# When weights are converted and gated-unit blocks are issued, in a fused attention, gated unit and soft mixture kernel

## The chip, the cores and the metric

The kernel runs on one core of a Trainium2 chip. The metric is the device time of one execution in microseconds, lower is better. Before the change the median of three runs is 917.54 us (913.38 to 921.64).

## The reference, cut to what matters

Four batches of eight heads: queries are averaged in pairs along the sequence, then ordinary attention follows. Its output is the input of a gated unit, and that feeds a soft mixture of eight small networks.

```python
q_pool = q.reshape(B, H, S // 2, 2, D).mean(axis=3)        # 4, 8, 576, 64
scores = scale * q_pool @ k.T                              # 576 x 1152 for each head
attn = softmax(scores); x = attn @ v                       # 2304 tokens x 512
g = x @ w_gate; h = g * sigmoid(g) * (x @ w_val)           # 512 -> 1536
y = h @ w_out                                              # 1536 -> 512
logits = y @ phi                                           # 2304 x 32 slots
# softmax over tokens gives slot inputs, over slots gives the combination
slot_out = relu(slot_input @ w1[e]) @ w2[e]                # 8 networks, 512 -> 1024 -> 512
out = softmax(logits, axis=1) @ slot_out
```

The weights of the gated unit arrive as 64-bit floats; the kernel turns them into 32-bit and then into a pair of 16-bit numbers (a high and a low part).

## The kernel before, in words

**Attention.** The heads are worked in 16 pairs, counted here from 0 to 15 as in the code (`steps`; four pairs make a batch). For each pair the keys, queries and values are loaded (`load_pair`, line 168), split into 16-bit high and low parts and put in place by transfers of SP's queue (`split_pair`, line 210: QD, KK, QQ, KL, QH). The row maxima of a pair's scores are found during the pair before it: PE computes scores once (line 323), DVE reduces them (lines 329, 338, 341), and one transfer of ACT's queue brings them into QH (line 347). Then each of 21 units computes scores in PE (lines 413, 414), ACT takes the exponential (line 419), POOL or DVE subtracts the high half to get the low half PL (line 426), and PE multiplies with the values (lines 457 to 459). Which PL goes to DVE, and which unit stays in 32 bits, is given for each pair by `DVE_PART` (line 33, six entries) and `F32_PART` (line 51, five entries). At the end of each head `finish` normalises (line 487), and `turn` sends the pair's result through a transposing transfer (line 528) into the operand xT of the gated unit. The buffer `xhl` between the two is single. xT of block j lies in place j mod 4 (`xt_tile`, line 466), so that block 5 takes over the place of block 1.

**The gated unit** works in nine blocks of 256 tokens (`moe_stream`, line 924), each in six slices of 256 columns of the weights (`block_slice`, line 671): 48 matmuls on PE, 16 each on lines 685, 689 and 690, then ACT and DVE for the activation, and small matmuls for the logits. A block can start when its tokens are ready (two blocks after each batch of four pairs), a slice when its weights are converted (`moe["w"]`).

**The conversion** has 36 portions (`prep`): 12 of w_out (`prep_wo`, line 613) and 24 of the other two weights (`prep_w`, line 647). Each loads its part by SP's queue, ACT does two steps (lines 600, 601), and DVE assembles the bits (line 603). A portion of w_out is also stored, transposed in PE and multiplied with phi; a portion of the other two is cast in ACT (line 653) and its low half subtracted in POOL, for the first three in DVE (line 655). A set of six portions makes one slice of weights ready. When the last is issued, three loads of 1024 KB follow (line 902).

**What sets the order.** The program is written out in full by Python loops; the main loop goes through the steps of a pair (42 of them) and after each one issues what is due: maxima, then slices of the gated unit up to a pace, then portions of the conversion up to a pace. A scheduler then orders the instructions of each engine by these priorities; within an engine and within SP's queue they run in that order. The paces are the subject of the change. A block counts 31 parts (`QPB`). If the weights or tokens for the next part are not there, the loop goes on, and the parts are made up for as soon as they are. Six blocks are issued beside attention and three after it; then come the slot networks and the output.

Of the kernel before, what the change touches and what calls it, by code (L numbers as in the profile page):

```python
# [45 lines left out]
MOE_LEAD = 6  # L46
PB, LAG = 6, 3
MOE_START = 4
N_MOE = 6.1
PREP_BEG, PREP_END = 1, 7  # L50
F32_PART = [0.17, 0.0, 0.17, 0.25, 0.33]
VRB = 2
HNB = 1
# [11 lines left out]
def tile_pool_attention_glu_softmoe(  # L65
# [35 lines left out]
    def ps(tag, shape, dtype=F32, bufs=1, name=None):  # L101
        return psum.tile(shape, dtype, tag=tag, bufs=bufs, name=name or tag)
# [50 lines left out]
    steps = [(b, p) for b in range(B) for p in range(NP)]  # L153
# [14 lines left out]
    def load_pair(b, p):  # L168

        r = slice(D if (b, p) == steps[0] else 0, P)  # L170
        kr = at.tile([P, S], F32, tag="kraw", bufs=1, name=f"kr{b}_{p}")
        nc.sync.dma_start(out=kr[r], in_=kT[b, p, r])
        qr = at.tile([P, 2, SQ], F32, tag="qraw", bufs=1, name=f"qr{b}_{p}")
        nc.sync.dma_start(out=qr[r], in_=qT[b, p, r])
        vr = at.tile([P, 2, NCH, D + 1], F32, tag="vraw", bufs=VRB, name=f"vr{b}_{p}")
        nc.sync.dma_start(out=vr, in_=vP[b, p])
        raw[b, p] = (kr, qr, vr)
# [179 lines left out]
    def later(n, fn):  # L357

        due.append((now[0] + n, fn))

    def tick(n=1):
        now[0] += n
        while True:
            run = [d for d in due if d[0] <= now[0]]
            if not run:
                return
            due.remove(run[0])
            run[0][1]()
# [18 lines left out]
    def maxima(n):  # L387
        while n_rm[0] < min(n, MX0 + MXP * (len(steps) - 1)):
            next(maxs)
            n_rm[0] += 1  # L390
# [488 lines left out]
    def load(n, mark=None):  # L879
        key = order[n]  # L880
        ts = place(n, "_".join(map(str, key)))
        m = NQ // len(ts)

        piece[key] = [ts[e // m][:, e % m] for e in range(NQ)]
        for i, t in enumerate(ts):
            if key[0] == "w2":
                _, z, g, c = key
                k = HALF // ZW[z]
                t = t.rearrange("p e (c d) -> p e c d", c=k)
                for e in range(m):  # L890
                    src = w2[NQ * g + i * m + e, c * P:(c + k) * P, Z0[z]:Z0[z] + ZW[z]]
                    dma = nc.sync.dma_start(out=t[:, e], in_=src.rearrange("(c p) d -> p c d", p=P))
                    if mark and e >= Y5E:
                        after(dma, mark)
                continue
            if key[0] == "wo":
                src = wo_d[key[1] * NQ * P:(key[1] + 1) * NQ * P, :].rearrange("(c p) d -> p c d", p=P)
            else:
                e = slice(NQ * key[1] + i * m, NQ * key[1] + (i + 1) * m)
                src = w1[e, key[3] * P:(key[3] + 1) * P, key[2] * HALF:(key[2] + 1) * HALF]  # L900
                src = src.rearrange("e p f -> p e f")
            dma = nc.sync.dma_start(out=t, in_=src)
            if mark:
                after(dma, mark)
# [51 lines left out]
    moe_work = moe_stream()  # L956
    UNITS = 2 * (2 * NCH + 3)
    QPB = 5 * (NF // 2) + 1
    n_moe = QPB * N_MOE / (len(steps) - MOE_START)
    n_done = 0  # L960
    for i, (b, p) in enumerate(steps):
        for u, _ in enumerate(attn(b, p)):
            tick()
            f = (u + 1) / UNITS
            if u == (SPLIT0 if i == 0 else 0):
                if i + 1 < len(steps):
                    split_pair(*steps[i + 1])
                if i + 2 < len(steps):
                    later(0 if i == 0 else LOAD_LAG, lambda k=i + 2: load_pair(*steps[k]))

            if i:
                maxima(MX0 + MXP * i + int(MXP * min(1.0, max(0.0, f - MX_BEG) / (MX_END - MX_BEG))))
            else:
                maxima(9 + int((MX0 - 9) * min(1.0, f / MX0_END)) + int(MXP * min(1.0, max(0.0, f - MX1_BEG) / (MX1_END - MX1_BEG))))
            while i >= MOE_START and n_done < (i + f - MOE_START) * n_moe:
                if not next(moe_work, False):
                    break
                n_done += 1
            while prep and n_prep - len(prep) < (i + f - PREP_BEG) * n_prep / (PREP_END - PREP_BEG):
                prep.pop(0)()  # L980
                if not prep:
                    for n in range(NEE):
                        load(n)
# [25 lines left out]
    t = ps("st", [P, NF // 2, 2, NS], bufs=STB, name="gt")  # L1009
# [7 lines left out]
    t = ps("mm", [P, DM], bufs=MMB, name="si4p")  # L1017
# [11 lines left out]
    t = ps("tr", [P, ND, NS], bufs=TRB, name="siTp")  # L1029
# [44 lines left out]
    for g in range(E // NQ):  # L1074
        for h in range(2):
            t = ps("st", [P, HALF], bufs=STB, name=f"hp{g}_{h}")
# [9 lines left out]
            t = ps("mm", [P, NQ, P], bufs=MMB, name=f"hTp{g}_{h}")  # L1086
# [119 lines left out]
```

## Time and profile before

| | |
|---|---|
| median of three runs | 917.54 us |
| profiled execution | 913.91 us, span 912.1 us |
| granted TensorE clock, mean | 0.964 |
| busy: PE, DVE, POOL, ACT | 823.9, 579.6, 444.5, 357.5 us |
| bytes moved | 134.69 MB, 148 GB/s |

Busy time is the time in which an engine had an instruction in work; matmuls overlap each other, so a busy PE is not a PE at its peak. The granted clock is a share of 2.4 GHz; a mean below 1 means that for part of the stretch the engine ran at 1.2 GHz. A stretch of a pair is counted here from the start of the last normalisation of the pair before it (line 487) to that of its own; the last one, of pair 15, starts at 722.3 us.

### The profile page before, as it was taken

The numbers are of one execution on the slowest core, as the hardware profiler recorded it, in microseconds if no ns is written. First come the engines' busy times: TensorE is split into PE (matmuls) and PEld (weight loads), VectorE is DVE, ScalarE is ACT, GpSimd is POOL, SyncE is SP. The second block draws the span as 40 slices with busy tenths as digits, with TensorE's granted clock in tenths as the row PEclk, the third lists the DMA queues.
The fourth block names the chain that finished last, engine by engine and source line by source line (L and its number), as shares of the span: only waits on it lengthen the run. The fifth ranks groups of instructions, "written<-read, shape, count | busy, mean of one in ns | idle before, by whom it ended". The sixth has DMA issues, their size and how long they took to land.

```text
span 912.1 us, 23728 instructions
## 1 busy us (share of the span) xinstructions
PE 823.9 (90%) x9954; PEld 582.6 (64%) x9954; DVE 579.6 (64%) x1083; ACT 357.5 (39%) x682; POOL 444.5 (49%) x384
## 2 busy tenths in 40 slices
PE   3869789899887899999999998989999999998897
PEld 1445466577655577676767675767677787676445
DVE  6878677764987356677867775786672454444313
ACT  2437576664756233332433334224333322112112
POOL 8646685736689422835765677257556400000100
PEclk9989799799999899999999999999999999999999
DMA  6558858665878612615262625142411199248999
GB/s 174 157 137 232 180 161 246 156 200 131 258 185 249 177 52 25 167 25 143 56 156 42 168 45 136 36 108 38 83 25 37 37 292 333 56 140 204 280 291 290
DMA packets 154267, 134.69 MB, mean 148 GB/s; under 512 B 83632, under 2 KB 123120, under 8 KB 154160
## 3 DMA queue, kind: packets, MB, share of 16 engines
q1 hardware_dynamic: 152000, 133.13, 55.5%
q8 instruction: 78, 1.28, 0.6%
q10 hardware_dynamic: 2160, 0.04, 0.1%
q14 instruction: 29, 0.24, 0.1%
HBM read 84.10 MB, written 7.86 MB: 101 GB/s over the span
## 4 chain that ended last, share of the span: by engine, by line
PE 68%; DVE 16%; DMA 10%; issue 2%; ACT 2%; SPq 1%; POOL 0%; DVEq 0%; ACTq 0%; POOLq 0%
PE st L414 6%; PE st L413 6%; PE mx L323 5%; PE g L685 5%; PE v L685 5%; PE g L689 5%; PE g L690 4%; PE v L690 4%; PE v L689 4%; DMA QH<-mt 4%; DVE mp L329 3%; PE pv L457 3%; PE pv L458 3%; PE pv L459 3%; PE hp L1079 2%
## 5 line engine op out<-in xcount | busy, mean ns | idle before, releaser
L426 POOL TENSOR_TENSOR PL<-P 128x512 f16<-128x512 f32 (+1 forms) x295 | 323.1, 1108 | 234.6 <-ACT P L419 231.3
L419 ACT ACTIVATE P<-st 128x512 f32<-128x512 f32 (+1 forms) x336 | 189.8, 581 | 237.2 <-PE st L414 179.0
L329 DVE TENSOR_REDUCE mp<-mx 128x1 f32<-128x512 f32 x270 | 179.2, 683 | 58.3 <-PE mx L323 57.1
L414 PE MATMUL st<-QH,KL 65*128 65x512 f16 (+1 forms) x576 | 148.3, 296 | 9.8 <-DMA QH<-mt 9.4
L413 PE MATMUL st<-QQ,KK 128*128 128x512 f16 (+1 forms) x576 | 147.7, 293 | 6.8 <-ACT P L419 6.6
L457 PE MATMUL pv<-VV,P 128*128 128x65 f16 x1088 | 141.5, 194 | 1.1 <-DVE x L489 1.0
L458 PE MATMUL pv<-VV,P 128*128 128x64 f16 x1088 | 140.8, 196 | 0.0
L459 PE MATMUL pv<-VV,PL 128*128 128x65 f16 x1088 | 138.1, 193 | 3.0 <-DVE PL L426 2.7
L685 PE MATMUL g<-xT,wgv 128*128 128x256 f16 x432 | 120.1, 278 | 9.0 <-DVE hs L697 7.5
L323 PE MATMUL mx<-kh,QD 128*128 128x512 f16 x270 | 106.5, 414 | 22.0 <-DVE mp L329 12.7
L457 PEld LDWEIGHTS <-P 128*128 128x128 bf16 x1088 | 105.0, 99 | 24.5 <-issue 4.3
L689 PE MATMUL g<-xT,wgv 128*128 128x256 f16 x432 | 120.1, 278 | 0.0
L690 PE MATMUL g<-xT,wgv 128*128 128x256 f16 x432 | 120.0, 278 | 0.0
L685 PE MATMUL v<-xT,wgv 128*128 128x256 f16 x432 | 118.8, 275 | 0.2 <-DVE hs L697 0.2
L689 PE MATMUL v<-xT,wgv 128*128 128x256 f16 x432 | 118.5, 274 | 0.0
L690 PE MATMUL v<-xT,wgv 128*128 128x256 f16 x432 | 118.5, 274 | 0.0
L459 PEld LDWEIGHTS <-PL 128*128 128x128 f16 x1088 | 104.6, 100 | 19.1 <-DVE PL L426 3.5
L458 PEld LDWEIGHTS <-P 128*128 128x128 bf16 x1088 | 104.1, 99 | 12.0 <-issue 1.0
L685 PEld LDWEIGHTS <-wgv 128*128 128x128 f16 x864 | 86.0, 100 | 29.5 <-issue 6.9
L689 PEld LDWEIGHTS <-wgv 128*128 128x128 f16 x864 | 85.4, 99 | 21.6 <-issue 7.1
L690 PEld LDWEIGHTS <-wgv 128*128 128x128 f16 x864 | 85.5, 99 | 18.0 <-issue 0.8
L414 PEld LDWEIGHTS <-KL 65*128 65x128 f16 x576 | 52.8, 99 | 37.5 <-issue 23.2
(177 smaller groups left out, 1224.6 us busy)
## 6 DMA issues: line engine op xcount, KB each, us to landing
w<-in_w SPq DMA_DIRECT2D x16, 1024.0 KB, 7.6
w<-in_w SPq DMA_DIRECT2D x64, 256.0 KB, 5.4
vr<-in_vP SPq DMA_DIRECT2D x16, 585.0 KB, 6.2
KK<-kh SPq DMA_DIRECT2D x62, 144.0 KB, 3.3
qr<-in_qT SPq DMA_DIRECT2D x15, 576.0 KB, 5.8
kr<-in_kT SPq DMA_DIRECT2D x15, 576.0 KB, 4.7
r<-in_w_out SPq DMA_DIRECT2D x12, 512.0 KB, 4.1
r<-in_w_gate SPq DMA_DIRECT2D x24, 256.0 KB, 4.9
```

What stands on the lines that cost most here:

```text
L323: nc.tensor.matmul(t, q, kh[:, k0:k0 + kw], start=True, stop=True)
L329: nc.vector.reduce_max(out=mp[:, g, c:c + 1], in_=t, axis=AX.X)
L413: nc.tensor.matmul(t[:, o:o + w], KK[:, k], QQ[:, q0:q0 + w], start=True, stop=False)
L414: nc.tensor.matmul(t[:, o:o + w], KL[:, k], QH[:, q0:q0 + w], start=False, stop=True)
L419: marks.append(nc.scalar.activation(P32[:, :o], t[:, :o], AF.Exp, scale=1.0 / 16.0).ins.name)
L426: eng.tensor_tensor(out=PL[:, :o], in0=P32[:, :o], in1=PH[:, :o], op=ALU.subtract)
L457: nc.tensor.matmul(dst[:, :D + 1], PH[:, q], VV[:, c, 0, :], start=first, stop=False, skip_group_check=True)
L458: nc.tensor.matmul(dst[:, :D], PH[:, q], VV[:, c, 1, :D], start=False, stop=False, skip_group_check=True)
L459: nc.tensor.matmul(dst[:, :D + 1], PL[:, q], VV[:, c, 0, :], start=False, stop=(c == NCH - 1), skip_group_check=True)
L685: mm = nc.tensor.matmul(o, w[:, 0, d, f], xh, start=(d == 0), stop=False)
L689: nc.tensor.matmul(o, w[:, 0, d, f], xl, start=False, stop=False)
L690: nc.tensor.matmul(o, w[:, 1, d, f], xh, start=False, stop=(d == ND - 1))
```

## The change: two paces

The conversion's pace starts at pair 2 and ends with pair 7, where it started at pair 1 and ended with pair 6. It stays at six portions per pair. The gated unit's pace was 6.1 blocks in equal shares over pairs 4 to 15 (0.51 per pair); now one block is due over pairs 4 to 7 (0.25 per pair) and 5.1 over pairs 8 to 15 (0.64 per pair). What is computed, and the order within the gated unit and within the conversion, stay the same.

```diff
 MOE_START = 4
-N_MOE = 6.1
-PREP_BEG, PREP_END = 1, 7
+
+MOE_PACE = [(4, 0.0), (8, 1.0), (16, 6.1)]
+PREP_BEG, PREP_END = 2, 8
...
     QPB = 5 * (NF // 2) + 1
-    n_moe = QPB * N_MOE / (len(steps) - MOE_START)
+
+    def moe_due(t):
+        for (t0, m0), (t1, m1) in zip(MOE_PACE, MOE_PACE[1:]):
+            if t < t1:
+                return QPB * (m0 + (m1 - m0) * (t - t0) / (t1 - t0))
+        return QPB * MOE_PACE[-1][1]
+
...
-            while i >= MOE_START and n_done < (i + f - MOE_START) * n_moe:
+            while i >= MOE_START and n_done < moe_due(i + f):
```

## Rows read from the trace of the kernel before

**Rows 1.** The page's totals: engine, busy us, share of the span, instructions.
```profile
PE 823.9 (90%) x9954; PEld 582.6 (64%) x9954; DVE 579.6 (64%) x1083; ACT 357.5 (39%) x682; POOL 444.5 (49%) x384
```

**Rows 2.** Busy time by stretch: pairs 1 to 7, pair 11, 8 to 15, after.
```profile
core 0: us, PE busy (x) PEld busy (x) DVE busy (x) ACT busy (x) POOL busy (x), PEclk, DMA share, GB/s
...
57.40:98.80 41.40, 29.99 (x409) 18.73 (x408) 34.42 (x61) 26.68 (x50) 22.71 (x18) 0.87 0.64 175
98.80:141.60 42.80, 37.75 (x411) 23.91 (x411) 27.70 (x53) 26.89 (x53) 32.57 (x26) 0.80 0.71 177
141.60:175.00 33.40, 29.01 (x369) 19.34 (x362) 27.17 (x46) 22.76 (x45) 22.10 (x16) 0.88 0.84 230
175.00:226.20 51.20, 49.90 (x562) 38.68 (x562) 30.19 (x53) 30.14 (x57) 27.66 (x22) 0.98 0.64 171
226.20:261.60 35.40, 32.23 (x461) 22.96 (x460) 31.13 (x55) 23.04 (x46) 23.80 (x19) 1.00 0.67 204
261.60:311.10 49.50, 38.38 (x472) 25.51 (x472) 33.08 (x51) 27.29 (x53) 40.23 (x33) 0.92 0.87 241
311.10:369.50 58.40, 58.40 (x717) 44.47 (x716) 35.00 (x72) 17.23 (x35) 18.98 (x17) 0.98 0.24 48
510.80:550.40 39.60, 38.08 (x501) 27.42 (x499) 31.73 (x52) 15.47 (x29) 29.93 (x25) 1.00 0.46 109
369.50:722.30 352.80, 339.73 (x4401) 246.97 (x4400) 239.78 (x435) 126.67 (x241) 215.27 (x182) 0.99 0.35 82
722.30:845.00 122.70, 113.95 (x1051) 89.01 (x1051) 57.52 (x130) 24.43 (x48) 0.00 (x0) 0.99 0.72 198
```

**Rows 3.** Line 685 by stretch: pairs 4 to 7, pair 11, pairs 8 to 15.
```profile
175.00:226.20 51.20, 16.53 (x61) 6.11 (x61) 0.98 0.64 171
226.20:261.60 35.40, 5.24 (x20) 1.87 (x19) 1.00 0.67 204
261.60:311.10 49.50, 5.62 (x19) 2.09 (x20) 0.92 0.87 241
311.10:369.50 58.40, 26.66 (x96) 9.61 (x96) 0.98 0.24 48
510.80:550.40 39.60, 10.09 (x37) 3.51 (x36) 1.00 0.46 109
369.50:722.30 352.80, 107.82 (x391) 38.73 (x391) 0.99 0.35 82
```

**Rows 4.** The chain of waits within pair 1 (57.4 to 98.8 us), shares by line.
```profile
by line: DVE mp L329 18.7%; DVE r L603 11.9%; DMA QH<-mt 8.7%; PE st L414 7.1%; DVE PL L426 6.2%; DVE mp L338 5.7%; DMA QH<-qh 5.6%; PE mx L323 4.8%; PE st L413 4.7%; DVE wgv L655 4.6%; issue 3.7%; DVE kh L184 3.2%; DVE xhl L499 2.9%; PE wo
```

**Rows 5.** POOL's groups over the span: count, busy us, mean ns, idle before.
```profile
L426 POOL TENSOR_TENSOR PL<-P 128x512 f16<-128x512 f32 (+1 forms) x295 | 323.1, 1108 | 234.6 <-ACT P L419 231.3 <-PE pv L458 1.6 <-POOL PL L426 0.3
...
L236 POOL TENSOR_TENSOR kl<-kr,kh 128x1152 f16<-128x1152 f32 (+1 forms) x16 | 40.4, 2526 | 17.3 <-DVE kh L184 11.0 <-DMA QH<-qh 3.6 <-DVE rs L487 1.5
...
L655 POOL TENSOR_TENSOR wgv<-r,wgv 128x512 f16<-128x512 f32 x21 | 27.7, 1320 | 10.2 <-ACT wgv L653 10.2
```

**Rows 6.** Line 603 on DVE in pairs 2 and 6: busy us and count.
```profile
98.80:141.60 42.80, 4.68 (x6) 0.80 0.71 177
...
261.60:311.10 49.50, 6.83 (x5) 0.92 0.87 241
```

**Rows 7.** DVE's longest waits in pair 6 (261.6 to 311.1 us).
```profile
DVE qh L184 <- DMA QH<-qh: 6.9, 1, 6.9
DVE qr L227 <- DMA qr<-in_qT: 6.7, 1, 6.7
```

**Rows 8.** PE in the second block (start, us), and the logits' groups over the span.
```profile
341.79 0.27 PE L690 MATMUL v<-xT,wgv 128*128 128x256 f16 x1
...
343.10 0.27 PE L690 MATMUL v<-xT,wgv 128*128 128x256 f16 x1
...
L729 PE MATMUL lp<-hs,W2S 128*64 128x256 bf16 x108 | 18.0, 297 | 1.9 <-ACT hs L717 1.6 <-DVE xT L184 0.3
...
L734 PE MATMUL lp<-hs,W2S 128*32 128x256 f16 x108 | 16.8, 283 | 0.4 <-DVE hs L719 0.4
```

## The prediction

> **What bounds the kernel now.** I read the engines' totals first [rows 1]: PE is busy for 90% of the span and no other engine for more than 64%. That share is an average over stages with different limits, so I then cut the span into one stretch per pair of heads (0 to 15), from the start of one pair's last normalisation on line 487 to the next one's [rows 2]. The reader is to see three regimes there. In pairs 1 to 3 PE is idle for 11.4, 5.1 and 4.4 us and its granted clock is 0.87, 0.80 and 0.88: part of the time it ran at 1.2 instead of 2.4 GHz. These pairs hold attention and conversion and no matmul of the gated unit. In pairs 4 to 6 the conversion goes on beside some slices of the gated unit. From pair 7 on the conversion is over and PE is the bound: in pair 7 it is busy for all 58.4 us, in pairs 8 to 15 for 339.7 of 352.8.
>
> How much of the gated unit lies in each stretch is read from the matmuls of line 685, of which a slice (a sixth of a block) has 16 [rows 3]: 61, 20, 19 and 96 in pairs 4 to 7, that is 3.8, 1.25, 1.2 and 6.0 slices. The first block is held up by its weights, which come one slice per pair; the second then runs in one go in pair 7. Pairs 8 to 15 have 391/16 = 24.4 slices, and what is left of nine blocks of six, 17.4, comes after the last pair.
>
> In pair 1 the path that set the end runs through DVE, not PE [rows 4]: the bit assembly of the conversion (line 603) is 11.9% of the chain and its subtraction (line 655) 4.6%.
>
> **The change part by part.** The conversion keeps its 36 portions but starts and ends a pair later; the gated unit keeps its order and its total, and 6 of 12 slices of pairs 4 to 7 go to pairs 8 to 15. I sum against the profiled execution: span 912.1 us, its own time 913.9, which is 3.6 below the median 917.54.
>
> *Pair 1 loses the conversion.* With it go a sixth of everything: 12 transfers on SP's queue (two loads and two stores of w_out, eight loads of the other weights), ACT's two steps and its cast per portion, DVE's line 603, three subtractions and PE's transposes of w_out. The chain's 16.5% of 41.4 us is 6.8 us; with the ACT steps and transposes that stand in the same chain I take 8.0, which brings the pair to the 33.4 that pair 3 takes. Bounds: 0, if attention's own waits take its place, and 11.4, all of PE's idle time. Late next is attention's own DVE work, the maxima of line 329, already 18.7% of the chain.
>
> *Pairs 2 and 3* convert before and after. Pair 2 takes over the three subtractions that go to DVE, 4.6% of pair 1's chain or 1.9 us: between 0 and 1.9, taken as 1.
>
> *Pairs 4 to 7* took 51.2 + 35.4 + 49.5 + 58.4 = 194.5 us. Now each has a sixth of the conversion and 1.5 slices. A slice beside attention is priced by pair 7 against pair 11 [rows 2, 3], both without conversion: (58.4 - 39.6)/(6.0 - 2.3) = 5.1 us. Pair 4: 51.2 - 2.3 x 5.1 = 39.4. Pair 5: 35.4 + 0.25 x 5.1 = 36.7. Pair 6: 49.5 + 0.3 x 5.1 = 51.1, but it held a stall that moves: at the end of the conversion three 1024 KB loads go out, and the queue's and DVE's waits behind them are 6.9 and 6.7 us [rows 7]. PE was idle for 11.1 us there against 3.2 in pair 5, so 7.9 of it go with the stall: 43.2. Pair 7 gets the conversion in place of 4.5 slices, its 12 transfers between those of the next pair on SP, the stall too, and all of its PL subtractions on POOL, since the DVE shares of line 33 end at pair 5: 21 at 1.108 us, kl 2.5 and four wgv at 1.32 make at least 31.1 us of POOL [rows 5], as in pair 6. I take 47, midway between 43.2 and 51.1, since PE has a slice to run while the loads land. Together 166.3, a gain of 28.2. Bounds: pair 5's 35.4 four times (gain 52.9) and the second rival's below (gain 7.1).
>
> Line 603 shows what conversion costs next to a full POOL: 1.37 us each in pair 6, 0.78 in pair 2 [rows 6]. The Trainium skill (SBUF — State Buffer, section "SBUF: two separate sides") states an exclusive port pair for GpSimd and two-input VectorE operations, the loser waiting for a whole instruction; these rows agree. By it pair 7's six conversions would lose up to 6 x 1.108 = 6.6 us of DVE, an estimate that would put the pair at 51 and the sum 4 us higher.
>
> *Pairs 8 to 15* take 6 slices more. The floor is PE's own spacing: consecutive matmuls of the unit start 0.109 us apart (12 steps in 1.31 us [rows 8]), so 48 are 5.2 us; the logits' two rows add 34.8 us of busy time in 54 slices, 0.6 each. I take 5.8, so 34.8 us. Against it, PE is idle for 13.1 us in these pairs and an even 3.8 slices per pair leave fewer holes; I credit a quarter, 3.3. That makes +31.5. Bounds: 6 x 5.1 - 13.1 = 17.5, and the stretch after the last pair, where a slice with all its waits takes 122.7/17.4 = 7.05 us: 42.3. That stretch itself starts with six blocks done in both kernels; I cost it at nothing.
>
> Sum: -8.0 + 1.0 - 28.2 + 31.5 = **-3.7 us**: 910.2 against 913.9, or 913.8 against the median.
>
> *The wait that is new.* The second block now ends in pair 9 instead of pair 7, and its operand xT1 shares its place with block 5's, into which pair 8's transposes (line 528) write. By the pace they are issued 0.29 into pair 9, and the last matmuls of the block at 8 + (60/31 - 1)/0.6375 = 9.47: 0.18 of 44.1 us, 8 us late. Behind them on SP lie the loads of a pair that starts later; who waits is the cast into the single xhl buffer at about 9.6, and on DVE behind it the maxima. The margin is 0.13 of a pair, 6 us, more than a transpose takes. Cost between 0 and 8; taken as 0.
>
> **The rivals.**
> *Faster: every converting pair runs like pair 5.* There DVE is busy for 88% and PE for 91% of 35.4 us, with 1.25 slices and the conversion; the slices fill what the conversion leaves. Four times 36.7 is 146.8: sum -8.0 + 1.0 - 47.7 + 31.5 = -23.2, so 894. Against it: pairs 6 and 7 have POOL at 31.1 us or more, and pair 5 gives three tenths of its PL subtractions to DVE (line 33).
> *Slower: slices add to converting pairs instead of filling them.* Pairs 1 to 3, conversion with no slice, took 117.6/3 = 39.2 us with PE's matmuls broken up and the clock down to 0.80. With 1.5 slices on top, 46.85 each and 187.4 in all: sum -8.0 + 1.0 - 7.1 + 31.5 = +17.4, so 935. It decides when pairs 4 to 7 average over 42.5 us, where the sum is zero. For it: pair 6 with 1.2 slices has a clock of 0.92. Against it: 0.98 and 1.00 in pairs 4 and 5. The Trainium skill (TensorE: Matmul & The Clock Gate, section "HAM oscillation — how this bites in real kernels") says that a matmul stream broken by waits falls back to the low clock again and again; pairs 1 to 3 agree, pair 5 does not.
> *The xT1 wait is not covered:* +8, so 922.
> *Pair 1 gains nothing,* because its transfers of QH (14% of the chain with both [rows 4]) and PE's low clock take the freed time: +8, so 922.
>
> **How the numbers follow.** About 1%, 9.2 us, is what a measurement of this kernel can tell from no change. Forecast 0.42, around 914; the fast rival 0.24; the slow one 0.17; xT1 0.10; pair 1 0.07. Of the forecast's 0.42, by the bounds of the slice price, 0.10 is faster by over 1% and 0.02 slower; the fast rival gives 0.23 faster, the slow one 0.16 slower, the two small ones 0.04 slower. Faster 0.33, within 1% 0.45, slower 0.22. The range 896 to 932 leaves out about half of each large rival.
>
> **What would show it.** In the profile after: pair 1 at 33 to 34 us; pairs 4 to 7 with about 25 matmuls of line 685 each and 166 us in all; pairs 8 to 15 at 384 us with 30 slices; the loads of line 902 in pair 7 or 8; DVE waiting for a transfer out of xhl in pair 9 only if xT1 bites. I am wrong if pairs 4 to 7 average far from 41.6, or if pairs 8 to 15 grow by less than 20 or more than 42.

## The result, and the profile after

The changed kernel takes 910.17 us (median of 11 runs, 904.92 to 911.97) against 917.75 before (11 runs, 911.08 to 921.64): ratio 0.9908, 95% interval 0.9879 to 0.9937. Run again later, beside other kernels, it gave 0.9948 (0.9917 to 0.9980). So it is faster by half a per cent to one per cent. The profiled execution took 909.44 us, its span is 907.6: 4.5 us less than the profiled one before. The rest of the 7.6 us between the medians is not in these two traces, since the execution profiled before was one of the faster ones of its kernel.

The stretches of pairs 1 to 7 and of pairs 8 to 15, as in [rows 2] (length; busy time and count of PE, PEld, DVE, ACT, POOL; clock; DMA share; GB/s):

```profile
58.28:91.83 33.55, 27.68 (x381) 17.26 (x380) 26.43 (x49) 15.20 (x30) 21.53 (x18) 0.85 0.43 116
91.83:128.38 36.55, 28.63 (x383) 19.57 (x383) 27.44 (x48) 24.12 (x46) 25.59 (x21) 0.95 0.66 186
128.38:174.91 46.53, 38.68 (x398) 23.64 (x399) 35.65 (x56) 27.80 (x54) 28.35 (x21) 0.82 0.69 195
174.91:216.07 41.16, 39.32 (x468) 29.20 (x469) 25.88 (x46) 26.88 (x51) 25.95 (x20) 1.00 0.60 180
216.07:249.56 33.49, 31.20 (x468) 23.00 (x466) 31.11 (x55) 24.07 (x47) 24.13 (x19) 1.00 0.72 215
249.56:300.91 51.35, 45.17 (x508) 28.86 (x508) 35.59 (x61) 28.54 (x55) 39.18 (x34) 0.90 0.75 209
300.91:342.42 41.51, 33.00 (x456) 23.58 (x456) 29.98 (x45) 23.15 (x46) 33.65 (x28) 0.96 0.79 214
...
342.42:716.72 374.30, 371.47 (x4728) 275.00 (x4727) 241.74 (x469) 131.67 (x250) 205.06 (x175) 1.00 0.35 76
```

Line 685 is now 686 (from line 51 on, numbers up to the main loop are higher by one). Its matmuls in pairs 4 to 7 and in pairs 8 to 15, as in [rows 3]:

```profile
174.91:216.07 41.16, 8.72 (x32) 3.28 (x32) 1.00 0.60 180
216.07:249.56 33.49, 6.54 (x24) 2.34 (x24) 1.00 0.72 215
249.56:300.91 51.35, 6.42 (x24) 2.42 (x24) 0.90 0.75 209
300.91:342.42 41.51, 5.78 (x22) 2.15 (x22) 0.96 0.79 214
...
342.42:716.72 374.30, 131.56 (x483) 47.23 (x483) 1.00 0.35 76
```

The slices are where they were said to go: 2.0, 1.5, 1.5 and 1.4 in pairs 4 to 7, and 30.2 instead of 24.4 after. By stretch the time changed so:

| stretch | before | after | change | forecast |
|---|---|---|---|---|
| pair 0 | 57.4 | 58.3 | +0.9 | 0 |
| pair 1 | 41.4 | 33.6 | -7.8 | -8.0 |
| pairs 2 and 3 | 76.2 | 83.1 | +6.9 | +1.0 |
| pairs 4 to 7 | 194.5 | 167.5 | -27.0 | -28.2 |
| pairs 8 to 15 | 352.8 | 374.3 | +21.5 | +31.5 |
| after | 189.8 | 190.9 | +1.1 | 0 |

The two things to see: pairs 8 to 15 hold 5.8 slices more, but PE's idle time in them, its holes, fell from 13.1 to 2.8 us; and what pair 1 gained, pairs 2 and 3 lost. A row of this table comes from one execution on each side; in a later trace of the same changed kernel (after_again, below) pairs 2 and 3 took 82.1 us, pairs 4 to 7 170.7 and pairs 8 to 15 374.4, so rows can differ by 3 us from one execution to the next. The chain of waits within pair 1, against [rows 4], has lost the conversion; PE now leads it:

```profile
by line: PE st L415 16.7%; PE st L414 15.4%; PE mx L324 13.3%; DMA vr<-in_vP 11.1%; DMA QH<-mt 10.6%; PE pv L458 7.2%; PE pv L459 7.2%; PE pv L460 7.1%; PE pv L450 3.8%; PE mx_r L324 2.2%; DVE kh L185 2.0%; SPq L242 1.8%; PE tx L539 1.3%; D
```

### The profile page after: what moved, and what is told of

Its sections match the earlier page's. It is cut to its first block, busy times and chain, and to the rows that moved or that the text cites. A ratio compares the mean times of both kernels' runs of the same rounds, so it can differ in the third digit from the quotient of the medians.

```text
span 907.6 us, 23732 instructions
## 1 busy us (share of the span) xinstructions
PE 827.5 (91%) x9954; PEld 584.7 (64%) x9954; DVE 574.6 (63%) x1083; ACT 359.1 (40%) x682; POOL 443.2 (49%) x384
## 4 chain that ended last, share of the span: by engine, by line
PE 68%; DVE 15%; DMA 11%; issue 3%; ACT 2%; SPq 1%; POOL 0%; DVEq 0%; ACTq 0%
PE st L415 7%; PE st L414 6%; PE mx L324 5%; PE g L686 5%; PE g L691 4%; PE g L690 4%; PE v L686 4%; PE v L691 4%; PE v L690 4%; DMA qr<-in_qT 4%; DVE mp L330 3%; PE pv L458 3%; PE pv L459 3%; PE pv L460 3%; DMA QH<-mt 2%
## 5 line engine op out<-in xcount | busy, mean ns | idle before, releaser
L420 ACT ACTIVATE P<-st 128x512 f32<-128x512 f32 (+1 forms) x336 | 190.9, 581 | 256.3 <-PE st L415 218.8
L415 PE MATMUL st<-QH,KL 65*128 65x512 f16 (+1 forms) x576 | 150.9, 298 | 9.2 <-DMA QH<-mt 8.6
L324 PE MATMUL mx<-kh,QD 128*128 128x512 f16 x270 | 108.6, 418 | 20.4 <-DVE mp L330 8.8
L686 PE MATMUL g<-xT,wgv 128*128 128x256 f16 x432 | 118.7, 275 | 5.3 <-DVE hs L698 4.2
L691 PE MATMUL g<-xT,wgv 128*128 128x256 f16 x432 | 118.6, 274 | 0.0
L690 PE MATMUL g<-xT,wgv 128*128 128x256 f16 x432 | 118.4, 274 | 0.0
```

The source lines that it names most:

```text
L324: nc.tensor.matmul(t, q, kh[:, k0:k0 + kw], start=True, stop=True)
L415: nc.tensor.matmul(t[:, o:o + w], KL[:, k], QH[:, q0:q0 + w], start=False, stop=True)
L420: marks.append(nc.scalar.activation(P32[:, :o], t[:, :o], AF.Exp, scale=1.0 / 16.0).ins.name)
L686: mm = nc.tensor.matmul(o, w[:, 0, d, f], xh, start=(d == 0), stop=False)
L690: nc.tensor.matmul(o, w[:, 0, d, f], xl, start=False, stop=False)
L691: nc.tensor.matmul(o, w[:, 1, d, f], xh, start=False, stop=(d == ND - 1))
```

## The experiments

Each edit is against the changed kernel, and each kernel is named by the label of its expectation. Ratios are to the kernel before, with the 95% interval.

**1. The conversion's move alone (a_conv_only), and the pace alone (b_pace_only).**

```diff
-MOE_PACE = [(4, 0.0), (8, 1.0), (16, 6.1)]
+MOE_PACE = [(4, 0.0), (16, 6.1)]
```

> Only the conversion is moved (pairs 2 to 7); the gated unit keeps its even pace of 6.1 blocks over pairs 4 to 15. The weights then come so late that pairs 4 to 7 can hold at most the first block, as in the changed kernel, and the second block falls into pair 8 in one go. Theory (the gain is PE work moved from pair 7 into idle PE time of pairs 8 to 15, plus converting pairs that are all filled): pairs 4 to 7 at 167 us as in the changed kernel (167.5), pairs 8 to 15 at 374 to 381, the burst leaving holes that the even pace fills; ratio to the kernel before 0.990 to 0.998. Rival 1, the even pace is what counts: pairs 8 to 15 at 385 or more, ratio 1.00 or above. Rival 2, the move of the conversion is all of it: ratio 0.991, as the changed kernel.

```diff
-PREP_BEG, PREP_END = 2, 8
+PREP_BEG, PREP_END = 1, 7
```

> Only the gated unit's pace is changed; the conversion stays in pairs 1 to 6. Theory: pairs 1 to 3 at 117.6 us as before (the changed kernel has 116.6 there, since what pair 1 gained pairs 2 and 3 lost), pairs 4 to 7 at 160 to 168 us, pairs 8 to 15 at 374; ratio 0.985 to 0.994, so the pace alone gives the whole gain. Rival, the conversion's move is needed: pair 1 keeps its 8 us more and pairs 4 to 7 gain no more than 20, ratio 0.996 or above.

The first took 1.0128 (1.0086 to 1.0171), the second 0.9877 (0.9837 to 0.9917). The conversion's move alone makes the kernel slower; the pace alone gives the whole gain. Stretches of the first kernel, pair 8 and pairs 8 to 15, then line 686 in pair 8:

```profile
345.39:430.24 84.85, 84.58 (x969) 64.39 (x967) 49.47 (x104) 22.09 (x45) 18.21 (x16) 1.00 0.25 51
...
345.39:733.09 387.70, 373.35 (x4740) 274.59 (x4738) 251.49 (x473) 131.40 (x251) 204.98 (x175) 0.99 0.33 73
...
345.39:430.24 84.85, 43.66 (x160) 15.68 (x159) 1.00 0.25 51
```

This separates the evenness from the amount. Pairs 8 to 15 hold 30 slices as in the changed kernel, and PE is busy there for 373.4 us against 371.5; but 10 slices fall into pair 8 alone, and the eight pairs together keep 14.3 us of holes against 2.8. Of the 13.4 us between 387.7 and 374.3, 11.5 are holes. Rival 1 holds; my ratio was too low. Pairs 4 to 7 took 172.8 us here, 5.3 more than in the changed kernel, where I had expected no difference. Pairs 4 to 7, 8 to 15 and 1 to 3 of the second kernel:

```profile
172.97:338.52 165.55, 151.18 (x1907) 107.66 (x1907) 114.71 (x193) 93.78 (x181) 114.33 (x94) 0.95 0.66 184
338.52:710.78 372.26, 368.86 (x4700) 272.77 (x4698) 243.44 (x470) 131.03 (x248) 205.79 (x177) 1.00 0.35 78
57.38:172.97 115.59, 92.83 (x1181) 60.36 (x1181) 94.45 (x158) 76.02 (x147) 79.41 (x60) 0.89 0.71 196
```

Each of the three is within 2.1 us of the changed kernel's 167.5, 374.3 and 116.6, as the theory had it.

**2. How much belongs into the converting pairs.** Conversion in pairs 1 to 6, and half a block, or one and a half, due by pair 8.

```diff
-PREP_BEG, PREP_END = 2, 8
+PREP_BEG, PREP_END = 1, 7
-MOE_PACE = [(4, 0.0), (8, 1.0), (16, 6.1)]
+MOE_PACE = [(4, 0.0), (8, 0.5), (16, 6.1)]   # f_half
+MOE_PACE = [(4, 0.0), (8, 1.5), (16, 6.1)]   # g_more
```

> Conversion in pairs 1 to 6; half a block due in pairs 4 to 7 and 5.6 in pairs 8 to 15. About three slices fewer in pairs 4 to 7 than in b_pace_only. Pairs 8 to 15 have only 3.4 us of idle PE time left there. Theory (slices in converting pairs fill idle PE time, and no holes are left in pairs 8 to 15): pairs 4 to 7 shorten by 4 to 10 us only, pairs 8 to 15 grow by 15 to 19; ratio to the kernel before 0.995 to 1.003, slower than b_pace_only. The wait for the place of xT1: the second block now ends 1.1 pairs after pair 8's transposes are due, so DVE must show a wait for a transfer out of xhl in pair 9 or 10, worth 5 to 30 us more if it reaches PE. Rival (a slice costs the same in every pair): the ratio stays at 0.988.

> Conversion in pairs 1 to 6; one block and a half due in pairs 4 to 7 and 4.6 in pairs 8 to 15. Theory (an even load that leaves no hole is what counts; 1.5 blocks still leave pair 8 its 4 slices or fewer): pairs 4 to 7 about 174 to 182 us, pairs 8 to 15 355 to 363 with 4 to 9 us idle; ratio 0.986 to 0.996, no better than one block. Rival (converting pairs still have idle PE time, 14 us in b_pace_only, to be filled by more slices): ratio 0.980 to 0.985.

Half a block gave 1.0017 (0.9991 to 1.0043), one and a half 0.9956 (0.9937 to 0.9976); one block has 0.9877. Pairs 8 to 15 of the first, and of the second:

```profile
330.30:726.75 396.45, 384.25 (x4812) 284.21 (x4811) 244.60 (x468) 133.62 (x255) 206.38 (x177) 0.99 0.34 75
```

```profile
352.68:715.53 362.85, 352.74 (x4512) 257.65 (x4510) 242.24 (x448) 129.47 (x247) 213.58 (x182) 0.99 0.37 81
```

Pairs 4 to 7 shortened by 9.4 us with half a block and grew by 11.0 with one and a half. A slice in a converting pair thus costs 3.6 to 3.7 us, by the counts of line 686 (4.4, 7.0 and 10.1 slices in pairs 4 to 7). In pairs 8 to 15 both have more holes (12.2 and 10.1 us) than one block (3.4). So 2.6 slices fewer in the converting pairs save 9.4 us and cost 24.2 later. Slices do partly fill converting pairs, and one block is the best of the three. But my theory for half a block, that no holes are left in pairs 8 to 15, fell. Each of pairs 8 to 14 has 3.9 to 4.4 slices, and PE still waits there for DVE, above all for the low half of attention's output (line 500) and for the row maxima:

```profile
PE tx L539 <- DVE xhl L500: 4.6, 5, 1.7
PE mx L324 <- DVE mp L330: 4.4, 4, 2.5
```

So an even load of four slices does not close the holes by itself. Why they close with one block and not with half a block is open. With half a block the wait for the place of xT1 shows: pair 8's two transposes (line 529, start and us) stand 39 us apart, and in pair 9 DVE's cast into xhl waits 2.6 us for one of them.

```profile
387.18 1.20 SPq L529 DMA_TRANSPOSE xT<-xhl  x1
426.09 1.23 SPq L529 DMA_TRANSPOSE xT<-xhl  x1
```

How much of the 12.2 us of holes comes from it was not separated. In the changed kernel the same pair of transposes takes 8.05 us in SP's queue, 6.4 of them a wait for PE, and no wait of DVE for it shows:

```profile
401.67 8.05 SPq L529 DMA_TRANSPOSE xT<-xhl  x2
```

**3. What the conversion costs in pairs 1 to 3.** All of it in pairs 4 to 7 (i_conv_4):

```diff
-PREP_BEG, PREP_END = 2, 8
+PREP_BEG, PREP_END = 4, 8
```

> The new pace, and the whole conversion in pairs 4 to 7 (nine portions per pair), so that pairs 1 to 3 have none. Six kernels so far took 114 to 118 us in pairs 1 to 3 whether these held two or three pairs' worth of conversion (c_shares 109). Theory (pairs 1 to 3 are held by attention's own waits, transfers and the low clock, and lose what the conversion gives back): 107 to 113 us. Rival (each pair's conversion costs 8 us, as pair 1 alone shows): 3 x 33.5 = 100 us or less. Pairs 4 to 7 pay for half as much conversion again: 175 to 190 us. Ratio to the kernel before 0.990 to 1.010.

It took 1.0122 (1.0071 to 1.0174), more than I had expected. Pairs 1 to 3 without any conversion:

```profile
57.61:91.66 34.05, 28.67 (x381) 17.63 (x380) 25.75 (x48) 14.29 (x28) 21.31 (x18) 0.80 0.43 102
91.66:125.52 33.86, 27.98 (x356) 18.25 (x357) 19.82 (x33) 14.76 (x27) 23.73 (x20) 0.85 0.37 91
125.52:153.45 27.93, 25.60 (x351) 18.35 (x352) 23.42 (x39) 15.33 (x29) 15.85 (x14) 1.00 0.55 144
```

95.8 us, so my theory fell and the rival holds: every pair pays. Before the change three pairs' worth cost 117.6 - 95.8 = 21.8 us, 7.3 each; after it two pairs' worth cost 116.6 - 95.8 = 20.8, 10.4 each. The same conversion is dearer in pairs 2 and 3 of the changed kernel: 83.1 - 61.8 = 21.3 us against 76.2 - 61.8 = 14.4. Pairs 4 to 7 took 181.2, as expected. What I had not expected is behind them: only 5 slices fit there, pair 8 got 6 and took 65.6 us, and pairs 8 to 15 took 397.7.

**4. Why it is dearer there.** The lists of shares moved along with it, both, or DVE's alone:

```diff
-DVE_PART = [0.3, 0.3, 0.0, 0.3, 0.0, 0.3]
+DVE_PART = [0.3, 0.3, 0.3, 0.0, 0.3, 0.0, 0.3]   # c_shares and h_dve_shift
-F32_PART = [0.17, 0.0, 0.17, 0.25, 0.33]
+F32_PART = [0.17, 0.0, 0.0, 0.17, 0.25, 0.33]    # c_shares only
```

> The changed kernel, and the two lists of shares (which PL subtraction goes to DVE, which unit stays in 32 bits) moved one pair later with the conversion: DVE 0.3, 0.3, 0.3, 0, 0.3, 0, 0.3 and 32 bits 0.17, 0, 0, 0.17, 0.25, 0.33. Theory (pair 3 took 46.5 us after the change, 33.4 before, because its shares were fitted to another mix, with DVE at 35.7 of 46.5 us): pairs 2 and 3 fall from 83.1 to 76 us, pairs 6 and 7 gain some from DVE's share in pair 6, ratio to the kernel before 0.980 to 0.988. Rival (pairs 1 to 3 are held by transfers and the low clock, whatever the shares): pairs 2 and 3 at 80 to 86, ratio 0.988 to 0.995.

> The changed kernel with only DVE's list of shares moved one pair later (in c_shares the list of 32-bit units was moved too; pairs 2 and 3 took 76.4 us there and 83.1 in the changed kernel). Theory (pair 3 is long for DVE, which has its share of PL subtractions there beside the conversion: 35.7 us busy): pairs 2 and 3 at 75 to 78. Rival (the 32-bit units of pair 3 are what is long): 81 to 84. Either way pair 6 falls to about 40, and what of it reaches the end is open: ratio to the kernel before 0.982 to 0.993.

Ratios 0.9916 (0.9891 to 0.9941) and 0.9892 (0.9862 to 0.9922). Pairs 2, 3 and 8 of the first; then pairs 2 and 3 together of the second and of a_conv_only, whose code and lists for these pairs are those of the changed kernel:

```profile
91.14:127.09 35.95, 27.21 (x401) 17.89 (x401) 31.55 (x52) 25.22 (x47) 23.76 (x19) 0.95 0.68 193
127.09:167.48 40.39, 32.02 (x385) 21.22 (x386) 27.65 (x48) 23.40 (x47) 30.05 (x24) 0.86 0.61 169
...
326.74:390.72 63.98, 63.12 (x705) 44.59 (x704) 38.90 (x71) 20.31 (x39) 28.98 (x25) 0.92 0.33 88
```

```profile
92.10:172.81 80.71, 63.89 (x781) 42.31 (x781) 57.95 (x100) 51.94 (x100) 50.86 (x40) 0.92 0.71 198
...
91.88:172.57 80.69, 65.71 (x781) 42.65 (x782) 63.05 (x101) 51.58 (x100) 53.69 (x41) 0.89 0.68 194
```

With both lists moved pairs 2 and 3 take 76.3 us, what they took before the change, so the loss of 6.9 there comes from the lists meeting another pair, as far as one trace shows it. With DVE's list alone they take 80.7, in neither of my two ranges, and five traces with this conversion and unmoved lists (a_conv_only and j_qh2 among them) have 80.7 to 83.5: DVE's list alone shows no gain. The list of 32-bit units is needed for it; whether it is enough by itself was not run. None of the gain reached the end: pair 8 took 64.0 us against 52.3, at a clock of 0.92 and with one slice more, and the stretch after pair 15 3.2 us more.

**5. What makes pairs 6 and 7 long.** The three large loads written at pair 10 instead of behind the last portion, to put them off (d_wo_late); then, on the kernel with the pace alone, a share of pair 6 for DVE (e_pair6):

```diff
             while prep and ...:
                 prep.pop(0)()
-                if not prep:
-                    for n in range(NEE):
-                        load(n)
+            if i == 10 and u == 0:
+                for n in range(NEE):
+                    load(n)
```

> The changed kernel with the three 1024 KB loads that follow the conversion issued at pair 10. The prediction put 7.9 us of pair 6's length down to the stall behind these loads and moved part of it to pair 7. By that: pairs 6 and 7 together 4 to 8 us shorter than the 92.9 of the changed kernel, ratio to the kernel before 0.982 to 0.987. Rival (pair 6 is long for its full POOL, and the loads only fill time that is lost anyway): pairs 6 and 7 within 2 us of 92.9, ratio 0.989 to 0.993.

```diff
-PREP_BEG, PREP_END = 2, 8
+PREP_BEG, PREP_END = 1, 7
-DVE_PART = [0.3, 0.3, 0.0, 0.3, 0.0, 0.3]
+DVE_PART = [0.3, 0.3, 0.0, 0.3, 0.0, 0.3, 0.3]
```

> The new pace with the conversion in pairs 1 to 6 (as in b_pace_only, ratio 0.988 to the kernel before), and DVE takes three tenths of pair 6's PL subtractions. Putting off the three large loads left pair 6 at 51.5 us, so they are not what makes it long. Theory (POOL with all PL subtractions and the conversion's own sets pair 6's length): pair 6 falls from 45.3 us to 36 to 41, as pair 5 and as pair 6 did with DVE's share in c_shares (39.3), and 3 to 8 us of it reach the end: ratio 0.979 to 0.985. Rival (pair 6 is shorter only to hand its work to the next pairs): pairs 6 to 8 together within 2 us of the 131.8 of b_pace_only, ratio 0.986 to 0.990.

The first gave 0.9937 (0.9906 to 0.9968), with 51.5 and 41.4 us in pairs 6 and 7 against 51.4 and 41.5. But it does not test the loads: their place in the program was moved, and their place in SP's queue stayed. The first and the last of the three (start and us), in the kernel before, in the changed kernel and in d_wo_late:

```profile
278.64 0.39 SPq L902 DMA_DIRECT2D wo<-wo_d  x1
...
301.87 0.38 SPq L902 DMA_DIRECT2D wo<-wo_d  x1
```

```profile
312.46 0.53 SPq L903 DMA_DIRECT2D wo<-wo_d  x1
...
336.20 0.39 SPq L903 DMA_DIRECT2D wo<-wo_d  x1
```

```profile
312.97 0.53 SPq L903 DMA_DIRECT2D wo<-wo_d  x1
...
336.53 0.40 SPq L903 DMA_DIRECT2D wo<-wo_d  x1
```

So d_wo_late is the changed kernel once more, and neither its theory nor its rival was tested; where expectations further down say that the loads were put off, that is wrong. These rows still answer half of the question. Before the change the loads went out in pair 6 (261.6 to 311.1 us); after it they go out in pair 7 (300.9 to 342.4), and pair 6, now without them, still takes 51.4 us. So they are not what makes pair 6 long. Whether they lengthen pair 7 is open. There DVE waited 8.5 us, and SP's queue shows what the transfer that it waited for stood behind, a transfer into KK that waits for PE's scores of the pair that still uses that buffer:

```profile
DVE qh L185 <- DMA QH<-qh: 8.5, 1, 8.5
...
SPq L244 <- PE st L415: 4.9, 1, 4.9
```

The share for DVE: 0.9873 (0.9842 to 0.9903), my ratio being too low. Pairs 6 and 9 without it (b_pace_only), and with it; then two stretches of 5 us in pair 9 with it:

```profile
257.07:302.35 45.28, 40.60 (x522) 28.64 (x520) 30.72 (x52) 25.17 (x49) 34.60 (x29) 0.96 0.91 244
388.78:435.87 47.09, 46.59 (x595) 34.41 (x594) 32.66 (x71) 16.27 (x32) 26.67 (x23) 1.00 0.44 100
```

```profile
257.70:295.68 37.98, 33.79 (x469) 24.14 (x468) 30.51 (x51) 22.67 (x45) 25.81 (x20) 0.96 0.76 219
...
382.71:434.91 52.20, 49.47 (x595) 35.58 (x594) 34.37 (x71) 16.19 (x32) 26.38 (x22) 0.93 0.44 92
...
390.00:395.00 5.00, 2.59 (x35) 1.82 (x36) 4.13 (x7) 0.32 (x1) 2.27 (x2) 0.79 1.09 178
395.00:400.00 5.00, 5.00 (x34) 2.76 (x33) 1.58 (x4) 1.12 (x2) 1.04 (x1) 0.52 0.00 0
```

Pair 6 fell from 45.3 to 38.0 us and POOL's busy time in it from 34.6 to 25.8, so POOL's load is what made it long, and pairs 6 to 8 kept 6.7 us of that. It was given back in pair 9 (52.2 against 47.1, a stall of PE and then the low clock) and after, so the ratio stayed. The changed kernel with DVE's list moved (h_dve_shift) shows the same from both sides: there pair 5 loses DVE's share of the PL subtractions and pair 6 gets it. Its pairs 5 and 6, which took 33.5 and 51.4 us in the changed kernel:

```profile
211.68:253.56 41.88, 38.43 (x501) 26.67 (x502) 34.58 (x57) 27.53 (x54) 34.07 (x28) 0.96 0.85 232
253.56:288.06 34.50, 30.46 (x447) 22.65 (x446) 31.00 (x46) 21.12 (x42) 24.39 (x18) 0.95 0.57 172
```

**6. Two buffers for qh,** in the changed kernel (j_qh2), and with the conversion in pairs 1 to 6 (k_qh2_pace); and the changed kernel beside them (after_again).

```diff
-        qh = at.tile([P, SQ], F16, tag="qh", bufs=1, ...)
+        qh = at.tile([P, SQ], F16, tag="qh", bufs=2, ...)
-PREP_BEG, PREP_END = 2, 8      # k_qh2_pace only
+PREP_BEG, PREP_END = 1, 7
```

> The changed kernel with two buffers for qh. In pair 7 DVE waits 8.5 us with the cast into qh, until the transfers that read the old qh have run, and these stand on SP behind a transfer into KK that waits 4.9 us for PE; the prediction had put such a stall down to the three large loads, and putting these off left it (8.4 us). Theory (the single buffer is the cause): the wait is gone, pair 7 falls from 41.5 us to 34 to 38, ratio 0.983 to 0.988. Rival (DVE then waits at the next step for the same transfers, or the time is given back in pair 8): pairs 7 and 8 together within 2 us of 93.8, ratio 0.989 to 0.993.

> The new pace, the conversion in pairs 1 to 6, and two buffers for qh. b_pace_only (ratio 0.988) shows no wait of DVE for that buffer. If the buffer matters only through that wait: ratio within 0.003 of 0.988. If two buffers also let the splitting of pairs run ahead elsewhere: 0.980 to 0.984.

> The changed kernel itself, beside k_qh2_pace and j_qh2 on one chip. Its ratio was 0.991; 0.988 to 0.994 again. If k_qh2_pace then stands at 0.988 or below beside it, the conversion's move gives nothing or costs up to 0.3%; if the two stand the other way round, it gives a little.

The first: 0.9924 (0.9893 to 0.9955). The wait for qh is gone; DVE waits at the next step, for ql, instead. Pairs 7 and 8, and that wait:

```profile
296.50:340.25 43.75, 33.71 (x459) 22.87 (x458) 31.66 (x51) 23.56 (x47) 34.93 (x28) 0.97 0.73 204
340.25:395.77 55.52, 55.52 (x661) 40.40 (x660) 34.03 (x66) 18.54 (x37) 27.20 (x23) 0.96 0.29 67
...
DVE ql L235 <- DMA QQ<-ql: 6.1, 2, 5.4
```

99.3 us for the two pairs against 93.8: more than the rival's range, and nothing gained, for the reason that the rival names. With the pace alone the two buffers gave 0.9837 (0.9789 to 0.9884), 901.20 us, the lowest median measured; beside it the changed kernel gave 0.9948 (0.9917 to 0.9980), just above what I had expected.

Whether the second buffer adds anything to the pace is open, as the intervals of 0.9877 and 0.9837 overlap. That the conversion's move is not needed is shown twice: without it the ratio is 0.9877 against 0.9908 and 0.9948 with it, and with two buffers 0.9837 against 0.9924, where the two intervals do not overlap and the move is a loss.

## Why the prediction was right, and which steps were not

The forecast of 913.8 us, just under the kernel before, came out at 910.2. Its form was right: a large gain in pairs 4 to 7 and a loss of nearly that size in pairs 8 to 15. Two terms were off, by 6 and 10 us, in opposite directions; that the spans of the profiled executions differ by 4.5 us, against 3.7 forecast, is luck. And the whole gain belongs to the gated unit's pace, while the sum counted on 8 us from the conversion's move, which brought none in the end.

- *Pair 1* came out at 33.6 as forecast, and without conversion it is 34.0 in another kernel. The rival in which it gains nothing is out.
- *Pairs 2 and 3, taken as +1,* were mis-sized: +6.9. I looked only for instructions that move between these pairs and found three subtractions. What moved was the conversion against the two lists of shares; with both lists moved too, the loss is gone.
- *Pairs 4 to 7* gained 27.0 against 28.2, but with two errors in it. Pair 6 took 51.4 us, not 43.2: the step that put 7.9 us of it down to the stall behind the three loads failed. The loads left the pair for pair 7, as forecast, and PE's idle time in it fell from 11.1 to 6.2 us, but PE's busy time rose from 38.4 to 45.2, and the pair stayed as long. A share of its PL subtractions for DVE took 7.3 us off it in the kernel with the pace alone. The reading behind that step was wrong too: both rows of [rows 7] are waits of DVE, none is one of SP's queue. Pair 7 took 41.5, not 47. A DVE wait of 8.5 us like that of pair 6 did appear there, behind a transfer into KK that waits for PE. And a slice in these pairs, taken at 5.1 us from two pairs without conversion, costs 3.6 to 3.7 beside it (experiment 2).
- *Pairs 8 to 15* were mis-sized. A slice costs PE 5.5 us there, (371.5 - 339.7)/5.8, near the 5.8 taken. But I credited a quarter of the 13.1 us of holes, and 10.3 were filled. Experiment 1 shows that it needs the even load: with the same number of slices in a burst the holes stay. Experiment 2 shows that an even load is not all, since with half a block 12.2 us of holes stay at four slices per pair. The time lay within my bounds of 17.5 and 42.3.
- *The slow rival* needed more than 42.5 us in each of pairs 4 to 7 and gave them 46.9; they took 41.9, and 42.7 in after_again, so its price is out, if not by much at the bound. Pairs 4, 5 and 7 ran at a clock of 0.96 to 1.00; pair 6 ran at 0.90, so there the low clock can be part of the length. *The fast rival* needed every pair like pair 5; pair 6 was not, for POOL, as the argument against it said.
- *The xT1 wait* was there, 8.05 us in SP's queue where 8 were forecast late, and covered, as taken. With half a block it bit.
- Line 604 (603 before) took 7.63 us for 5 in pair 7, 1.53 each, where the prediction has 1.37 in pair 6 and 0.78 in pair 2:

```profile
300.91:342.42 41.51, 7.63 (x5) 0.96 0.79 214
```

By its share of busy time POOL was hardly fuller in pair 6 of [rows 2] (40.2 of 49.5 us) than in pair 2 (32.6 of 42.8), so that contrast of the prediction shows little. Single instructions of pair 7 show more (DVE, then POOL):

```profile
313.02 0.69 DVE L604 SCALAR_TENSOR_TENSOR r<-r 128x512 uint32<-128x512 uint32 x1
...
322.29 2.60 DVE L604 SCALAR_TENSOR_TENSOR r<-r 128x512 uint32<-128x512 uint32 x1 [1.32 <-ACT r L602]
```

```profile
321.95 2.38 POOL L237 TENSOR_TENSOR kl<-kr,kh 128x1152 f16<-128x1152 f32 x1
```

At 313.02 POOL had nothing in work (its next instruction starts at 313.55), and line 604 took 0.69 us. At 322.29 POOL was in a subtraction that ends at 324.33, and line 604 ended 0.56 us after it. The Trainium skill's rule on the port pair (SBUF — State Buffer, section "SBUF: two separate sides") agrees with these rows. Against 0.69 each the five lost 4.2 us, where the estimate by the rule had up to 6.6. But the pair took 41.5, not the 51 that the estimate made of it (47 and 6.6 would even be 53.6): DVE was idle for 11.5 us of it, so the time lost on line 604 need not have lengthened the pair.

## What to carry to other kernels

When work is moved into a stretch where one engine is nearly always busy, price it by that engine's time less the holes that the load can fill, and look at the load of each step, not the sum: the same 30 slices cost 374 us evenly spread and 388 with a burst. How many holes an even load leaves has to be measured: 3 us in one of these kernels, 12 in another. An instruction that is moved in the program need not move on its queue, and only the trace tells: the three large loads of experiment 5 did not. When work moves against a table that is indexed by step, the table is part of the change. A gain in the middle of a pipeline is worth only what the next stretches do not give back, and here two such gains, in pairs 2 and 3 and in pair 6, were given back.

## What was not expected of the hardware

A short stall of PE cost about twice its length here. Pair 9 of the kernel with DVE's share in pair 6 holds as many matmuls (595) as pair 9 of the kernel without it. In it PE is idle for 2.4 of the 5 us from 390 on, 2.0 of them in one wait for DVE's maxima (line 330). In the next 5 us PE counts as busy throughout, but the granted clock is 0.52, mostly the 1.2 GHz level: the same matmul takes 0.41 us there and 0.27 us after it.

```profile
396.56 0.41 PE L690 MATMUL v<-xT,wgv 128*128 128x256 f16 x1
...
400.00 0.27 PE L690 MATMUL v<-xT,wgv 128*128 128x256 f16 x1
```

In all the pair has 2.2 us more of idle time and 2.9 more of busy time, 5.1 together. The Trainium skill (TensorE: Matmul & The Clock Gate, section "HAM oscillation — how this bites in real kernels") tells of such a loss after waits, and these rows agree.
